# Weight slots returned to the front, rows scaled on ScalarE, and a fourth usual pair in a two-layer transformer kernel

## The chip, the cores and the metric

The kernel runs on one core of one Trainium2 chip. The metric is device time in microseconds (us) of one execution, median of the runs; lower is better.

## The reference

Two layers, each an attention block and then a gated block, on 2048 rows of 448 numbers, all in float32:

```python
x = A_x
x = x + attention(layernorm(x), wqkv, wo)          # 16 heads of 28
x = x + gated(layernorm(x), w_gate, w_up, w_down)
x = x + attention(layernorm(x), wqkv, wo)
x = x + gated(layernorm(x), w_gate, w_up, w_down)

def gated(x, w_gate, w_up, w_down):                # 448 -> 1792 -> 448
    return (sigmoid(x @ w_gate) * (x @ w_up)) @ w_down
```

The change touches the gated block of both layers, and only there its schedule.

## The kernel before

TensorE works in float16: each operand is split into a high and a low float16 part, and a product is the sum of three (high by high, low by high, high by low). The schedule is written out by hand: each engine executes its instructions in the order in which the program emits them, and the tile framework adds the waits between engines.

**The gated block.** The 2048 rows are cut into `NB = 4` blocks of 512, the 1792 hidden features into `NP = 7` pairs of 2 x 128. The loop `for b, p in seq` in `gated` runs over the 28 pairs of a layer, (0,0) to (3,6). For a pair `gate_and_up` computes gate and up products with a fast 2x2 scheme of seven products instead of eight: `first`, `second`, `third` write the two `chain` banks, which ScalarE copies out (`on_chain`, L1527); `apart` and `c11_c22`, `c12` write the two `side` banks, which VectorE adds (L1543, L1550); `c21` uses the chain banks again. In between stand six places, `along(0)` to `along(5)`, to which the list `at` assigns other work: the operands of the pair before (`Operands.parts`, `rest`), the down products of the block before (`pieces`), and preparation steps of a later block (`run_fill(steps, n)`, counts from `portions(b, p)`). 78 matmuls of 256 columns make a pair.

**The down product** uses the same scheme: seven products per pair, for block `b - 1` while block `b` goes through its pairs; in one pair of block b that is six matmuls of 224 columns for each pair of the block before. The last block's products follow in a stage of their own after the loop (the order is `TAIL`); it will be called the closing stage. The first `USUAL` pairs of block 0 go another way: their down product is done in the usual form (`down`, 24 matmuls of 448 columns, banks 0 to 3), emitted behind the next pair, and `add_usual` adds it to `x`. So TensorE's order in block 0 is pair 0, pair 1, down of 0, pair 2, down of 1, and so on.

**Preparing a block.** `Block.steps()` lists it: `norm` (mean and variance on VectorE, the power on GpSimd), `squares` (VectorE scales the rows and transposes 32x32 squares), `store` and `gather` (through DRAM, to complete the transpose, by SyncE's queue), and nine half steps `r11` to `last_rows`, in which VectorE subtracts and ScalarE rounds to float16. Block b + 1 is prepared in block b. In the first layer, the last block prepares two blocks for the next attention (`after`).

**Slots.** Large tiles take one of 19 equal slots of SBUF (`big`), quarter-sized ones one of 12 (`qrt`). `get` takes the slot at the front of the list of free ones, `put` appends the slot at its end. A tile whose slot had another tile before it waits for that tile's last reader. `WeightsGated` keeps two pairs of gate/up weights (two tiles of 800 KB each per pair, `load_gu`) and three tiles of down weights (784 KB, `load_dn`). `used_gu` and `used_dn`, called at the end of each pair (in the closing stage `used_dn` after each product), put the used slots and start the next load on GpSimd's queue. The closing stage begins like this; the load of the fourth product's weights is started by the first `used_dn` of the second loop:

```python
for n in range(3):
    pieces(b, TAIL[n], range(NP - 1), w[n], True)
for n in range(3):
    pieces(b, TAIL[n], [NP - 1], w[n])
    wt.used_dn()
    finish(b, TAIL[n])
for k in TAIL[3:]:
    ...
        pieces(b, k, range(NP), wt.dn[0])
```

Of the kernel before, what the change touches and what calls it, by code (L numbers as in the profile page):

```python
# [19 lines left out]
P = 128  # L20
S = 2048
D = 448
# [34 lines left out]
N_SUMS = 25  # L57
DN = D // 2
N_DN = 8
USUAL = 3  # L60
SHORT = ((10, 23, 12), (11, 24, 13), (8, 22, 9))
# [13 lines left out]
class Slots:  # L75
# [28 lines left out]
    def put(self, *tiles):  # L104
        for t in tiles:
            i, _ = self.held.pop(id(t))
            self.free.append(i)


@with_exitstack  # L110
def interleaved_layers(ctx: ExitStack, tc: tile.TileContext, x_in, wqkv, wo, w_gate, w_up,
# [143 lines left out]
    class Block:  # L255
# [15 lines left out]
        def norm(self, js=range(TB)):  # L271
            b = self.b
            if js[0] == 0:
                uid[0] += 1
                self.mv = cpool.tile([P, TB, 2], F32, name=f"mv_{uid[0]}", tag="mv", bufs=2)
                self.rs = cpool.tile([P, TB], F32, name=f"rs_{uid[0]}", tag="rs", bufs=2)
            for j in js:
# [6 lines left out]
                                    op1=ALU.mult)  # L284
            nc.gpsimd.tensor_tensor(rs, rs, nhalf[:, c], op=ALU.pow)

        def scale(self, j):
# [34 lines left out]
        def gather(self):  # L322
            rows = self.scr.rearrange("j r i n -> (j r) (i n)")
            self.raw = big.get("xraw", [P, 4, W])
            nc.sync.dma_start(self.raw[:, 0:3, :],
                              rows[0:384].rearrange("(k p) n -> p k n", p=P))
            nc.sync.dma_start(self.raw[0:64, 3, :], rows[384:D])
            if self.halves:
                nc.gpsimd.memset(self.raw[64:P, 3, :], 0.0)

# [12 lines left out]
        def steps(self):  # L343
            return self.squared() + [
                lambda: (self.store(), self.gather())] + (
                        self.half_steps() if self.halves else
                        [lambda: self.ready(0, 1), lambda: self.ready(2, 3)])

        def squared(self):
            return [lambda do=do, j=j: do((j,)) for do in (self.norm, self.squares)  # L350
                    for j in range(TB)]

        def half_steps(self):
# [43 lines left out]
            def r11():  # L397
                self.wide = big.get("xwide", [P, 4, 2, 2, W // 2], F16)
                self.short = big.get("xshort", [P, 3, 2, 2, W // 2], F16)
                self.t1 = subtract("t1", cut(0, 2), cut(0, 0))  # L400
                high(self.wide[:, 0], cut(0, 0))
# [51 lines left out]
        def begin(self):  # L453
            uid[0] += 1
            self.mv = cpool.tile([P, TB, 2], F32, name=f"mv_{uid[0]}", tag="mv", bufs=2)
            self.rs = cpool.tile([P, TB], F32, name=f"rs_{uid[0]}", tag="rs", bufs=2)
            self.xn = big.get("xn", [P, TB, D])
# [870 lines left out]
    class WeightsGated:  # L1328
# [26 lines left out]
        def load_dn(self, queue=nc.sync):  # L1355
            self.dn.append(big.get("dn", [P, NP, 2, DN], F16))
            queue.dma_start(self.dn[-1], dn_parts[self.products.popleft()])

        def used_gu(self):
            big.put(*self.gu.popleft())  # L1360
            if self.pairs:
                self.load_gu(nc.gpsimd)

        def used_dn(self):
            big.put(self.dn.popleft())
            if self.products:
                self.load_dn(nc.gpsimd)

    def gated(layer, first, wt, before_next):
# [237 lines left out]
        for b, p in seq:  # L1607
            if p == 0:
                if b + 1 < NB:
                    blks.append(Block(b + 1, True))  # L1610
                    steps.extend(blks[b + 1].steps())
                elif not last:
                    after = [Block(0), Block(1)]
                    blks.append(after[0])
                    steps.extend(after[0].steps())
# [12 lines left out]
            for i, n in enumerate(portions(b, p)):  # L1628
                at[i].append(lambda n=n: run_fill(steps, n))
            if b == 0 and p > USUAL or b == 1 and p == 0:  # L1630
                for j in range(TB)[p - USUAL - 1:p - USUAL] if b == 0 else range(
                        NP - USUAL - 1, TB):
                    at[0].append(lambda j=j: add_usual(j))
# [160 lines left out]
```

## Time and profile before

| | |
|---|---|
| median of 3 runs | 1913.93 us (1912.98 to 1913.96) |
| the profiled execution | 1918.24 us, its span 1916.4 us |
| TensorE clock in it | 0.997 of full speed |
| gated block, first layer, blocks 0 to 2 | from 605.6 to 850.3 us of the span |
| gated block, second layer, blocks 0 to 2 | from 1550.0 to 1796.4 us of the span |
| end of the second layer's closing stage | 1912.7 us of the span |

Times in the profile are microseconds from the span's start. PE is TensorE's matmuls, PEld its weight loads, DVE VectorE, ACT ScalarE, POOL GpSimd, SP SyncE; L545 is line 545 of the kernel. A matmul's duration covers its way through the array; the next one starts long before its end, so what one costs is the distance between starts. Pair boundaries are the first weight load of a pair on `gu_s`, counted off 78 to a pair; all 4368 are in the trace.

### The profile page before, as it was taken

What the parts mean: (1) busy time and instruction counts of PE and PEld (TensorE: products, weight loads), DVE (VectorE), ACT (ScalarE), POOL (GpSimd) and SP (SyncE); (2) the same over time, 40 slices, a digit from 0 to 9 for tenths busy, and PEclk for the clock granted to TensorE, in tenths of its full rate; (3) what the DMA queues carried; (4) which work ended last, traced back from release to release, by engine and by line L of the source; (5) the groups of instructions that cost most, each with busy time, mean ns of one, the idle gap of its engine ahead of it and who ended that gap; (6) DMA issues with size and microseconds to landing.
All of it is one profiled execution on the core that took longest, in us unless ns stands there. A gap on an engine that the chain in (4) does not pass through costs nothing. (4 is left out here: it accounts for less than half of the span.)

```text
span 1916.4 us, 56353 instructions
## 1 busy us (share of the span) xinstructions
PE 1897.9 (99%) x24317; PEld 1405.8 (73%) x24317; DVE 1412.8 (74%) x2816; ACT 1366.0 (71%) x1742; POOL 240.6 (13%) x467
## 2 busy tenths in 40 slices
PE   9999999999999999999999999999999999999999
PEld 4455655555566798999954568778888777899998
DVE  7648798687877598788663487778778667887764
ACT  5569999999983455454344799999999645555541
POOL 2013312232001111212100000000000011211110
PEclk9999999999999999999999999999999999999999
DMA  5575555345313657656634312122111235665752
GB/s 173 165 207 162 155 157 149 117 144 149 92 62 92 235 189 263 219 221 236 232 94 132 89 51 51 28 51 51 41 37 66 75 98 215 216 270 198 270 204 90
DMA packets 107298, 275.20 MB, mean 144 GB/s; under 512 B 12766, under 2 KB 63086, under 8 KB 106912
## 3 DMA queue, kind: packets, MB, share of 16 engines
q0 software_dynamic: 33088, 165.74, 24.5%
q1 hardware_dynamic: 73616, 105.54, 19.3%
q8 instruction: 192, 3.15, 0.7%
q14 instruction: 66, 0.54, 0.1%
q10 hardware_dynamic: 336, 0.23, 0.0%
HBM read 213.39 MB, written 50.73 MB: 138 GB/s over the span
## 5 line engine op out<-in xcount | busy, mean ns | idle before, releaser
L1144 ACT ACTIVATE prob_s<-sc 128x1536 f32<-128x1536 f32 x659 | 892.7, 1484 | 6.7 <-PE sc L1129 3.3
L1180 PE MATMUL acc<-prob_s,val_s 128*32 128x256 f32 (+3 forms) x7754 | 590.1, 383 | 0.0
L1129 PE MATMUL sc<-qp_s 114*32 114x512 f16 x7896 | 575.8, 379 | 0.0
L545 PEld LDWEIGHTS <-gu_s 128*128 128x128 f16 x4368 | 428.0, 98 | 60.3 <-issue 8.1
L1129 PEld LDWEIGHTS <-qp_s 114*32 114x32 f16 x8192 | 309.9, 96 | 176.3 <-issue 78.2
L1180 PEld LDWEIGHTS acc<-prob_s,val_s 128*32 128x32 f32 x7754 | 317.9, 110 | 100.8 <-issue 7.6
L545 PE MATMUL chain<-xwide_s,gu_s 128*128 128x256 f16 x2016 | 249.0, 273 | 4.1 <-DMA gu_s<-gu_parts 4.0
L1454 PE MATMUL dnp<-dn_s,hparts_s 128*128 128x224 f16 x2100 | 235.5, 259 | 0.0
L1454 PEld LDWEIGHTS <-hparts_s 128*128 128x128 f16 x2100 | 202.1, 98 | 4.8
L1527 ACT COPY one_q<-chain 128x256 f32<-128x256 f32 x224 | 82.0, 372 | 132.0 <-PE chain L545 131.3
L1160 DVE SCALAR_TENSOR_TENSOR power_q<-power_q,expo_q 128x512 f32<-128x512 f32 x222 | 153.7, 692 | 7.6
L545 PE MATMUL side<-xshort_s,gu_s 128*128 128x256 f16 x1120 | 142.1, 274 | 3.0 <-DVE one_q L1543 2.7
L530 PE MATMUL qkp<-xhl_s,wqk_s 128*128 128x512 f16 x616 | 138.0, 379 | 0.7 <-DVE xhl_s L509 0.3
L1543 DVE TENSOR_TENSOR one_q<-side,one_q 128x512 f32<-128x512 f32 x112 | 72.0, 684 | 83.4 <-PE side L545 83.4
L530 PEld LDWEIGHTS <-wqk_s 128*128 128x128 f16 x616 | 60.0, 98 | 70.1 <-ACT wqk_s L223 1.0
L1209 DVE STREAM_TRANSPOSE oturned_q<-acc 128x512 f32<-128x512 f32 x32 | 22.9, 717 | 118.4 <-PE acc L1180 118.4
L1345 POOL DMA_DIRECT2D gu_s<-gu_parts x104 | 56.0, 540 | 365.7 <-PE side L545 183.3
L545 PE MATMUL side<-xwide_s,gu_s 128*128 128x256 f16 x672 | 92.3, 274 | 0.0
L1407 ACT CAST hparts_s<-hsums_q 128x256 f16<-128x256 f32 (+1 forms) x144 | 68.4, 489 | 33.1 <-DVE hsums_q L1419 20.6
L722 ACT ACTIVATE qkhl_q<-qkp 128x512 f16<-128x512 f32 x56 | 33.2, 593 | 75.0 <-PE qkp L530 71.6
L1180 PE MATMUL acc<-power_q,val_s 128*32 128x256 f32 (+3 forms) x278 | 86.4, 393 | 0.0
L1554 ACT ACTIVATE one_q<-one_q 128x512 f32<-128x512 f32 x56 | 35.3, 630 | 71.3 <-DVE one_q L1543 71.2
(209 smaller groups left out, 2291.0 us busy)
## 6 DMA issues: line engine op xcount, KB each, us to landing
gu_s<-gu_parts POOLq DMA_DIRECT2D x104, 800.0 KB, 6.0
dn_s<-dn_parts POOLq DMA_DIRECT2D x50, 784.0 KB, 7.2
qp_s<-qk_scr SPq DMA_DIRECT2D x96, 224.0 KB
qk_scr<-qkhl_q SPq DMA_DIRECT2D x56, 256.0 KB
gu_parts<-pack_s POOLq DMA_DIRECT2D x14, 800.0 KB, 4.2
xt_scr<-xs_s SPq DMA_DIRECT2D x48, 224.0 KB
xraw_s<-xt_scr SPq DMA_DIRECT2D x12, 768.0 KB
qp_s<-qk_scr SPq DMA_DIRECT2D x64, 112.0 KB
```

What stands on the lines that cost most here:

```text
L530: nc.tensor.matmul(pm, w, x, start=(i == 0), stop=(i == len(terms) - 1))
L545: nc.tensor.matmul(pm, a, x, start=(first and i == 0), stop=(i == len(terms) - 1), skip_group_check=True)
L1129: nc.tensor.matmul(ps[32 * j:32 * j + 32, :], hd.k[:, keys], hd.q[:, qb * W:(qb + 1) * W], start=True, stop=True, tile_position=(0, 32 * j))
L1144: nc.scalar.activation(prob[:, 0:n, :], ps[:, 0:n, :], AF.Exp, scale=exp_scale)
L1160: nc.vector.scalar_tensor_tensor(p, p, c[k], y, op0=ALU.add, op1=ALU.mult)
L1180: nc.tensor.matmul(acc[qb * VC:(qb + 1) * VC, s], v[:, kc % TB, h, :], probs[c * NB + qb][:, s], start=(kc == 0 and a == 0), stop=(kc == N ...
L1345: queue.dma_start(self.gu[-1][m], gu_parts[p, m])
L1407: nc.scalar.copy(to[:, :, 0], a)
L1454: nc.tensor.matmul(pm, a[:, x, t], w[:, p, y], start=(begin and n == 0 and (j == 0 or alone)), stop=(n == 2), skip_group_check=True)
L1527: nc.scalar.copy(to, pm)
L1543: nc.vector.tensor_tensor(one[m], side[m], one[m], op=ALU.add)
L1554: nc.scalar.activation(out, v, AF.Sigmoid, scale=gate_scale)
```

## The change

It does five things.

- `put_next` puts slots back at the front of the free list; `used_gu` and `used_dn` use it, so that the next load of weights goes into the very slot just read.
- In the preparation VectorE no longer scales rows: `norm_one` adds two small GpSimd operations for an offset, `lift` has ScalarE compute scale times row plus offset into a quarter slot, and `square` has VectorE transpose it.
- Block 2's normalisation, transposition, `store` and `gather` move from block 1 to block 0's pairs; its half steps stay in block 1. Block 1's first half step moves from the second place of pair (0,2) to its last. `portions` is rewritten.
- `USUAL` is 4 instead of 3, with the times of `add_usual` in `AFTER_USUAL`. Block 1 then has three instead of four pairs of down products in each of its pairs, and the down weights for block 0 are loaded without their first four pairs.
- Two memsets on GpSimd move or go (`gather`, `t3`); `last_low` gets a small ScalarE copy of zeros.

```diff
-USUAL = 3
+USUAL = 4
+AFTER_USUAL = ((0, 5), (0, 5), (1, 0), (1, 2))
...
+    def put_next(self, *tiles):
+        for t in tiles[::-1]:
+            i, _ = self.held.pop(id(t))
+            self.free.appendleft(i)
...
+        def norm_one(self, j):
+            self.norm((j,))
...
+            nc.gpsimd.tensor_tensor(off, self.mv[:, j, 0:1], self.rs[:, j:j + 1], op=ALU.mult)
+            nc.gpsimd.tensor_scalar(off, off, -1.0, None, op0=ALU.mult)
+
+        def lift(self, j):
+            self.lifted[j] = qrt.get("lifted", [P, D])
+            nc.scalar.activation(self.lifted[j], x[:, self.b * TB + j, :], AF.Identity,
+                                 scale=self.rs[:, j:j + 1], bias=self.off[:, j:j + 1])
+
+        def square(self, j):
+            if j == 0:
+                self.xs = big.get("xs", [P, NQ, TB, 32])
+            if j + 1 < TB:
+                self.lift(j + 1)
+            v = self.lifted.pop(j)
+            nc.vector.transpose(self.xs[:, :, j, :], v)
+            qrt.put(v)
...
         def steps(self):
-            return self.squared() + [
-                lambda: (self.store(), self.gather())] + (
+            squared = self.squared()
+            return squared[:-1] + [
+                lambda: (squared[-1](), self.store(), self.gather())] + (
...
         def squared(self):
-            return [lambda do=do, j=j: do((j,)) for do in (self.norm, self.squares)
-                    for j in range(TB)]
+            return [lambda j=j: self.norm_one(j) for j in range(TB)] + [
+                lambda: self.lift(0)] + [lambda j=j: self.square(j) for j in range(TB)]
...
-                nc.gpsimd.memset(self.t4[64:P, 1, :], 0.0)
...
+                nc.scalar.copy(self.short[64:P, 1, 1, 1], self.raw[64:P, 3, 0:W // 2])
...
         def load_dn(self, queue=nc.sync):
-            self.dn.append(big.get("dn", [P, NP, 2, DN], F16))
-            queue.dma_start(self.dn[-1], dn_parts[self.products.popleft()])
+            t = big.get("dn", [P, NP, 2, DN], F16)
+            first = USUAL if len(self.products) > NP * (NB - 1) else 0
+            queue.dma_start(t[:, first:], dn_parts[self.products.popleft(), :, first:])
+            self.dn.append(t)

         def used_gu(self):
-            big.put(*self.gu.popleft())
+            big.put_next(*self.gu.popleft())
...
         def used_dn(self):
-            big.put(self.dn.popleft())
+            big.put_next(self.dn.popleft())
...
-        blks = [first]
-        steps = deque()
+        blks = [first] + [Block(b, True) for b in range(1, NB)]
+        s1, s2 = blks[1].steps(), blks[2].steps()
+        ahead = 2 * TB + 1
+        steps = deque(s1[:ahead] + s2[:TB] + s1[ahead:] + s2[TB:ahead])
...
         if b == 0:
-            steps = {0: {1: 4, 5: 5}, 2: {1: 1, 2: 1, 3: 1, 5: 1}, 3: {1: 1, 2: 1, 3: 1, 5: 1},
-                     4: {1: 1}}
-        elif b < NB - 1:
-            steps = {0: {1: 2, 2: 1}, 1: {1: 2, 2: 1}, 2: {1: 1, 2: 2}, 3: {5: 1},
-                     4: {1: 1, 3: 1}, 5: {1: 1, 3: 1}, 6: {1: 1, 2: 1, 3: 1, 5: 1}}
+            steps = {0: {1: 4, 3: 1, 5: 4}, 2: {1: 2, 2: 2, 5: 1}, 3: {1: 1, 2: 2, 3: 1, 5: 1},
+                     4: {1: 1, 2: 1, 3: 2, 5: 2}, 5: {1: 2}}
+        elif b == 1:
+            steps = {1: {1: 1, 5: 1}, 2: {2: 1}, 3: {1: 1, 5: 1}, 4: {5: 1}, 5: {1: 1, 5: 1},
+                     6: {2: 1}}
+        elif b == 2:
+            steps = {0: {1: 2, 2: 2}, 1: {1: 2, 2: 1, 5: 2}, 3: {2: 1, 5: 1}, 4: {1: 1, 5: 1},
+                     5: {1: 1, 2: 1, 5: 1}, 6: {1: 1, 3: 1}}
         else:
-            steps = {0: {1: 2, 2: 1}, 1: {1: 2, 2: 1}, 2: {1: 1, 2: 2}, 3: {1: 2, 2: 2},
-                     4: {1: 1, 2: 1}, 5: {1: 1, 2: 1}, 6: {1: 1, 2: 2, 5: 1}}
+            steps = {0: {1: 2, 2: 1}, 1: {1: 2, 2: 1}, 2: {1: 2, 2: 2}, 3: {1: 2, 2: 2},
+                     4: {1: 2, 2: 1}, 5: {1: 1, 2: 1}, 6: {1: 1, 2: 2, 5: 2}}
```

More of the change, by code (lines that the diff above doesn't have):

```diff
@@ L274, in norm @@
                 uid[0] += 1
-                self.mv = cpool.tile([P, TB, 2], F32, name=f"mv_{uid[0]}", tag="mv", bufs=2)
-                self.rs = cpool.tile([P, TB], F32, name=f"rs_{uid[0]}", tag="rs", bufs=2)
+                self.mv = cpool.tile([P, TB, 2], F32, name=f"mv_{uid[0]}", tag="mv", bufs=4)
+                self.rs = cpool.tile([P, TB], F32, name=f"rs_{uid[0]}", tag="rs", bufs=4)
             for j in js:
@@ L285, in norm @@
             nc.gpsimd.tensor_tensor(rs, rs, nhalf[:, c], op=ALU.pow)
+        def norm_one(self, j):
+            self.norm((j,))
+            if j == 0:
+                self.off = cpool.tile([P, TB], F32, name=f"off_{uid[0]}", tag="off", bufs=4)
+                self.lifted = {}
+            off = self.off[:, j:j + 1]
+            nc.gpsimd.tensor_tensor(off, self.mv[:, j, 0:1], self.rs[:, j:j + 1], op=ALU.mult)
[5 more added lines that the diff above has]
+        def square(self, j):
+            if j == 0:
+                self.xs = big.get("xs", [P, NQ, TB, 32])
[4 more added lines that the diff above has]
+            qrt.put(v)
         def scale(self, j):
@@ L399, in r11 @@
                 self.short = big.get("xshort", [P, 3, 2, 2, W // 2], F16)
+                if not self.turned:
+                    nc.gpsimd.memset(self.raw[64:P, 3, :], 0.0)
                 self.t1 = subtract("t1", cut(0, 2), cut(0, 0))
@@ L1608, in gated @@
             if p == 0:
-                if b + 1 < NB:
-                    blks.append(Block(b + 1, True))
+                assert b == 0 or not steps
+                if b == 1:
+                    steps.extend(s2[ahead:])
+                elif b == 2:
                     steps.extend(blks[b + 1].steps())
-                elif not last:
+                elif b == NB - 1 and not last:
                     after = [Block(0), Block(1)]
-                    blks.append(after[0])
                     steps.extend(after[0].steps())
@@ L1629, in gated @@
                 at[i].append(lambda n=n: run_fill(steps, n))
-            if b == 0 and p > USUAL or b == 1 and p == 0:
-                for j in range(TB)[p - USUAL - 1:p - USUAL] if b == 0 else range(
-                        NP - USUAL - 1, TB):
+            for j in range(TB):
+                if AFTER_USUAL[j] == (b, p):
                     at[0].append(lambda j=j: add_usual(j))
```

7 lines of the change are left out of this document (3 added, 4 removed).

## The prediction

> **What bounds the kernel now.** I read the page first, then the waits of TensorE, then busy times by pair of the gated loop.
>
> ```profile
> span 1916.4 us, 56353 instructions
> PE 1897.9 (99%) x24317; PEld 1405.8 (73%) x24317; DVE 1412.8 (74%) x2816; ACT 1366.0 (71%) x1742; POOL 240.6 (13%) x467
> PE chain L545 <- DMA gu_s<-gu_parts: 4.0, 2, 2.1
> PE chain L545 <- ACT one_q L1527: 3.6, 2, 2.5
> PE side L545 <- DVE one_q L1543: 2.7, 2, 2.0
> ```
>
> TensorE sets the time; nothing else can gain except where it waits or does less. Its long waits are few: weights that land late, and chain or side banks that ScalarE and VectorE free late, each once per layer. Where, and what they cost with all that follows, the busy times by stage tell (length, busy PE, PEld, DVE, ACT, POOL, granted clock, DMA share, GB/s):
>
> ```profile
> 627.36:645.50 18.14, 14.80 (x103) 10.57 (x102) 9.56 (x22) 6.74 (x16) 2.41 (x5) 0.91 0.43 149
> 645.50:658.56 13.06, 13.06 (x104) 9.98 (x103) 7.46 (x19) 7.55 (x20) 0.57 (x2) 1.00 0.79 292
> 658.56:667.15 8.59, 8.59 (x79) 7.62 (x78) 4.98 (x12) 4.68 (x13) 1.07 (x2) 1.00 0.78 317
> 684.20:762.48 78.28, 76.17 (x716) 69.39 (x714) 68.85 (x154) 43.58 (x108) 15.48 (x32) 1.00 0.63 223
> 727.89:740.85 12.96, 10.98 (x104) 9.86 (x103) 9.95 (x23) 6.44 (x16) 1.59 (x3) 1.00 0.76 298
> 740.85:762.48 21.63, 21.63 (x206) 19.84 (x205) 19.56 (x44) 14.23 (x35) 4.00 (x8) 1.00 0.61 230
> 1571.78:1589.93 18.15, 15.11 (x104) 10.51 (x103) 9.76 (x22) 6.73 (x16) 2.70 (x6) 0.91 0.42 151
> 1628.63:1708.66 80.03, 77.83 (x717) 70.27 (x715) 68.85 (x154) 43.58 (x108) 15.48 (x32) 0.98 0.63 224
> 1672.32:1687.03 14.71, 12.65 (x105) 10.72 (x103) 9.95 (x23) 6.44 (x16) 1.59 (x3) 0.88 0.68 265
> ```
>
> Rows 1 and 7 are pair (0,2) with the usual down product of pair 0 behind it, in the first and second layer; row 2 is the same work in pair (0,3), undisturbed: 5.1 us are lost per layer. Row 3 is a pair alone, 8.59. Rows 4 and 8 are the seven pairs of block 1. Two undisturbed pairs there take 21.63 (row 6), 10.82 each; seven would take 75.7, so 2.6 and 4.3 us are lost, mostly in pair (1,4) (rows 5 and 9). The same wait costs 2.1 us at full clock in row 5 and 3.9 in row 9, where the clock fell to 0.88: a lowered clock is worth about 1.75 us.
>
> The timelines of VectorE and GpSimd in the second layer show what (0,2) waits for.
>
> ```profile
> 1564.55 0.53 POOL L1345 DMA_DIRECT2D gu_s<-gu_parts  x1 [7.88 <-DVE xs_s L305]
> 1574.07 1.05 POOL L1345 DMA_DIRECT2D gu_s<-gu_parts  x2 [9.00 <-DMA xt_scr<-xs_s]
> 1578.52 0.76 DVE L371 TENSOR_TENSOR t_q<-xraw_s 128x256 f32<-128x256 f32 x2 [8.15 <-DMA xraw_s<-xt_scr]
> 1581.67 0.42 DVE L371 TENSOR_TENSOR t_q<-xraw_s,t_q 128x256 f32<-128x256 f32 x1 [1.39 <-DMA xraw_s<-xt_scr]
> 1582.02 1.28 DVE L1543 TENSOR_TENSOR one_q<-side,one_q 128x512 f32<-128x512 f32 x2
> 1668.03 7.21 DMA gu_s<-gu_parts
> ```
>
> VectorE sits in `r11` until the rows of block 1 are back from DRAM, and only then frees the side bank. Weight loads wait for a slot that `xs` still holds; the last row (chain of waits) is such a load, landing at 1675.24 for pair (1,4), which began at 1672.32.
>
> **What the change takes away.** In (0,2), `r11` moves from the second place to the last, so nothing in that pair waits for the rows, and ScalarE doing the scaling sends them off earlier. Its next deadline is pair (0,3), a usual down product (4.5 us) later. I take the whole 5.1 per layer: **-10.2**. In block 1 three product pairs stand in each pair instead of four; six matmuls of 224 columns cost 0.57 (row below), so a pair falls from 10.82 to 10.25. With weights in their own slots no load waits for `xs`, whose work has also left block 1. Seven pairs: 71.7 instead of 78.3 and 80.0: **-14.9**.
>
> **What it adds on TensorE.** One more usual down product per layer, row 2 less row 3, 4.5 us: **+9.0**. The scheme with seven products is given up for that pair, so this trade alone costs 0.5 per layer.
>
> **Closing stage.** Here I look at what the old order of slots gave. Rows of the chain of waits, GpSimd's timeline and the down weights (last one: around 935 to 942 us):
>
> ```profile
> 1869.69 1.09 PE side L545 x10
> 1873.25 0.57 PE dnp L1454 x6
> 1883.33 29.34 PE dnp L1454 x306
> ...
> 1870.54 1.08 POOL L1357 DMA_DIRECT2D dn_s<-dn_parts  x2 [10.31 <-PE side L545]
> 1872.23 0.53 POOL L1357 DMA_DIRECT2D dn_s<-dn_parts  x1 [0.62 <-PE dnp L1454]
> ...
> DMA to landing us min/median/max: 4.4/6.6/7.4
> ...
> DMA to landing us min/median/max: 4.8/12.0/17.7
> ```
>
> The 306 matmuls of row 3 run without a gap: twelve belong to pair (3,6), the other 294 are the closing stage, 0.096 us each. Its weights were all on their way by 1872.23, twelve microseconds ahead, because `get` handed out slots that gate/up weights had left. With `put_next` the load for the fourth product takes the slot of the first, so it waits for the last reader of that: product 1's seventh pair. From there TensorE has twelve matmuls left, 1.15 us. The load is issued 0.3 after the last reader (five of row 1's ten matmuls end at 1870.24, the issue is at 1870.54) and takes 4.4 alone (the smallest of the three landings; the later two stood behind another). So TensorE waits 0.3 + 4.4 - 1.15, about 3.6 us per layer: **+7.2**. The fifth to seventh loads have a product of 42 matmuls (4.0) more cover each and land in time. In the first layer the next layer's weights move at the same time; the third product's load, issued at the stage's start, must land within 72 matmuls, 6.9 us. By the last two rows it takes between 4.4 and 12.0, a wait of 0 to 5.1; it is a single load, so I take **+0.5**.
>
> **ScalarE in pair (0,0).** Its last place now holds three `lift`s, emitted ahead of the two float16 copies for the down product and of the copy that frees chain bank 0 for the next pair.
>
> ```profile
> 1559.03 0.42 ACT L1554 ACTIVATE two_q<-two_q 128x256 f32<-128x256 f32 x1 [1.16 <-DVE two_q L1550]
> 1559.36 0.60 ACT L210 CAST hhl_q<-one_q 128x512 f16<-128x512 f32 x1
> 1559.94 0.62 ACT L210 CAST hhl_q<-two_q 128x512 f16<-128x512 f32 x1
> 1560.47 0.64 ACT L1527 COPY one_q<-chain 128x256 f32<-128x256 f32 x2
> ...
> L1407 ACT CAST hparts_s<-two_q 128x256 f16<-128x256 f32 x50 | 20.2, 404 | 0.0
> L223 ACT ACTIVATE wqk_s<-wraw_s,up 128x384 f16<-128x384 f32 x1 | 0.6, 599 | 0.0
> L223 ACT ACTIVATE wqk_s<-wraw_s,up 128x256 f16<-128x256 f32 x1 | 0.5, 507 | 1.2 <-DVE up L240 1.2
> L288 DVE TENSOR_SCALAR xn_s<-x,mv,rs 128x448 f32<-128x448 f32 x64 | 31.2, 498 | 4.8 <-POOL rs L285 3.5 <-POOL rs L466 1.0
> ```
>
> ScalarE has no idle time there, so every microsecond ahead of 1560.47 is TensorE's. No `lift` is in the trace. L223 scales by a per-row operand: 507 and 599 ns for 256 and 384 columns, by that slope 645 for 448; a second per-row operand (the offset) may add as much as the first did, 507 - 404, making 750. Instructions in a row start 0.08 before their predecessor ends. Three cost 1.7 to 2.0; I take 1.85 per layer: **+3.7**. They replace VectorE's 0.50 each, where VectorE was not what TensorE waited for. The Trainium skill (ScalarE: Activation LUTs, What ACT_TABLE_LOAD costs) gives about 93 ns for each such operand, and a lift would then take 745 ns, an estimate from that page; L223 agrees with 103 for one, and by the page the term is +4.0. The same page's Rules for kernel authors would leave multiply and add to VectorE, which speaks against this move, and the rows 498 against 645 to 750 agree.
>
> **Two half steps in one place of (0,3).** `t2` and `t3` both stand in the third place: VectorE's low part in `t3` needs ScalarE's high part of `t2`, which comes behind the copies of `third`.
>
> ```profile
> L381 ACT CAST xwide_s<-t_q 128x512 f16<-128x512 f32 x24 | 14.9, 620 | 6.6 <-DVE t_q L367 4.0 <-DVE t_q L371 2.5
> L390 DVE TENSOR_TENSOR xwide_s<-t_q,xwide_s 128x512 f16<-128x512 f32 x24 | 16.4, 682 | 0.0
> L371 DVE TENSOR_TENSOR t_q<-xraw_s,t_q 128x256 f32<-128x256 f32 x24 | 9.2, 418 | 1.7 <-DMA xraw_s<-xt_scr 1.7
> ```
>
> With matmuls of 256 columns at 0.109 (1.09 for ten, above), `third` ends 5.2 us into the pair, its copies at 5.8, the high part at 6.4 (0.62), the low part at 7.1 (0.68), `t4` at 7.8 (two of 0.42), and the side bank's sum 0.65 later, 8.4; `c12` would want it at 7.4. One microsecond per layer: **+2.0**; none, if ScalarE runs ahead of this count.
>
> **At nothing**, with cover: GpSimd's two more small operations per tile (13% busy), its memsets, the zero copy in `last_low` (ScalarE, places without a deadline), `lift`s in blocks 2 and 3 (pairs of 10 to 12.5 us, ScalarE busy about half), block 2's preparation in (0,4) and (0,5) (behind the extra down product), `add_usual` (VectorE, banks not needed before block 1 and later), GpSimd's load issue, now always behind the pair's end. In block 3 of the first layer `ready` comes one place earlier against its `gather`; up to 1.5 us if it lands late.
>
> **Sum of the waits**: -10.2 - 14.9 + 9.0 + 7.2 + 0.5 + 3.7 + 2.0 = -2.7.
>
> **The clock.** New waits of 3.6, 1.9 and 1.0 us per layer follow. Rows 5 and 9 show two waits of some 2.1 us, one with and one without the fall; rows 1 and 7 one with in each layer (0.91), after waits of more than 3 us together. So I count a fall for both closing stages, 1.4 each, since part of it passes in the wait, and one of the two after (0,0), 1.75: +4.55, and in all **+1.85**. The Trainium skill (TensorE: Matmul & The Clock Gate, The HAM clock gate) has the clock fall after an idle window of about 3.4 us; then these waits would hardly lower it, and the time would be that of case (e) below. Row 9 disagrees (a fall after 2.1 us), so I keep the rows.
>
> On the profiled execution that is 1918.24 + 1.85 = 1920.1 us; it stood 4.3 above the median, and the same difference on the median gives 1913.93 + 1.85 = **1915.8 us**. What a measurement can tell from no change is 0.2%, 3.8 us.
>
> **Rivals.** (a) Slower, by the clock: it falls after all four long waits, 1.75 each, +7.0 on -2.7: 1918.2. It leaves the 0.2% once clock falls cost over 6.5. For it speaks row 9, against it row 5. (b) Slower, by the weights: a load now starts only when its pair ends. In (0,6) the next must land in 8.6, plus 0.65 to the first use of the up half, less 0.5 for its later issue, 8.7 us. While rows went through DRAM two such loads took
>
> ```profile
> DMA to landing us min/median/max: 8.1/8.8/9.5
> ```
>
> and block 2's rows now travel just there. From 8.7 on it decides: 0.8 more and a fall of 1.75 per layer, +5.1 on the forecast: 1920.9. Against it: only the second of the two loads came that late. (c) Faster: the waits in (0,0) and (0,3) do not come, since ScalarE is idle earlier than I count: -2.7 - 5.7 and falls of 2.8 at the end: 1908.3. Against it speaks ScalarE's gapless row of 1559 to 1561. (d) The slots do not return as `put_next` says and the closing stage runs on: -2.7 - 7.7 + 1.75: 1905.3. (e) No fall at all: the sum of the waits alone, 1911.2; row 5 speaks for it, rows 1, 7 and 9 against.
>
> **Chances.** Forecast 0.33, (e) or part of the falls 0.10, (a) 0.22, (b) 0.15, (c) 0.13, (d) 0.07. Within 0.2% are the forecast and (e), 0.43; slower 0.37; faster 0.20. The forecast's own range is 1912 to 1918; with (a), (b), (c) and their open bounds (5.1 in the closing stage, 1.5 in `ready`) it is 1907 to 1923.
>
> **What would show it.** Right: pairs (0,2) near 13.1, block 1 near 10.25 per pair; a wait `PE dnp <- DMA dn_s` of about 3.6 in each closing stage; (0,1) longer by 1.9 behind L1527; (0,3) longer by 1.0 behind L1543; clock under 1 behind them. Wrong: a closing stage without a gap, which would leave the change faster, or waits for `gu_s` in blocks 0 and 1, which would make it clearly slower.

## Result and the profile after

The changed kernel takes 1931.65 us (median; 1930.14 to 1934.12), the kernel before beside it 1913.45 us: 1.0096 times as long, 95% interval 1.0079 to 1.0114. The forecast was 1915.8 us, in a range of 1907 to 1923. The profiled execution took 1934.12 us with a span of 1932.4, against a span of 1916.4 before: 16.0 us more. By the medians it is 18.2 us. The two profiled executions stood above their medians by different amounts (1934.12 against 1931.65, 1918.24 against 1913.93), so what follows adds up the 16.0 us between the two spans; which waits the median executions had more or less of, no trace shows.

Head of the page and top of TensorE's waits (us in total, times, longest):

```profile
span 1932.4 us, 56301 instructions
PE 1903.2 (98%) x24281; PEld 1321.0 (68%) x24281; DVE 1392.8 (72%) x2768; ACT 1386.3 (72%) x1772; POOL 253.8 (13%) x523
PE dnp L1492 <- DMA dn_s<-dn_parts: 11.8, 3, 4.1
PE side L579 <- DVE one_q L1581: 5.2, 5, 3.1
PE chain L579 <- ACT one_q L1565: 3.8, 2, 1.9
```

The busy time of VectorE fell by 20 us and that of ScalarE rose by 20, as the scaling moved from one to the other; neither total explains the longer time. The first wait is new: TensorE stands before a down product three times for weights, 11.8 us in all. Next, the stages that the prediction spoke of, from the busy times by stage (length, then busy time of PE, PEld, DVE, ACT, POOL, granted clock, DMA share, GB/s):

```profile
614.01:629.07 15.06, 13.14 (x105) 10.06 (x103) 10.92 (x24) 7.85 (x17) 3.08 (x6) 1.00 0.78 249
629.07:642.13 13.06, 13.06 (x104) 10.00 (x103) 7.62 (x19) 5.20 (x13) 5.69 (x18) 1.00 0.52 188
642.13:656.19 14.06, 13.27 (x104) 9.97 (x103) 8.90 (x20) 7.27 (x17) 1.06 (x2) 1.00 0.33 123
686.46:758.83 72.37, 72.10 (x675) 65.45 (x673) 62.49 (x138) 44.26 (x110) 12.22 (x23) 1.00 0.57 212
1645.00:1717.81 72.81, 72.10 (x675) 65.41 (x673) 62.50 (x138) 44.45 (x110) 12.23 (x23) 1.00 0.58 215
884.33:901.79 17.46, 14.36 (x122) 12.60 (x121) 11.10 (x25) 6.65 (x15) 5.28 (x16) 0.90 0.60 208
939.40:980.30 40.90, 33.00 (x298) 30.80 (x297) 8.69 (x16) 0.92 (x2) 2.64 (x5) 0.87 0.49 188
1893.40:1928.60 35.20, 31.26 (x297) 29.72 (x294) 8.65 (x16) 0.93 (x2) 2.64 (x5) 0.90 0.40 148
```

Rows 1 to 3 are pairs (0,1), (0,2) and (0,3) of the first layer: the wait of 5.1 us in (0,2) is gone (13.06), (0,1) is 1.87 longer than the 13.19 it had before (the row below), (0,3) 1.0 longer. Rows 4 and 5 are block 1 in both layers, 72.4 and 72.8 instead of 78.3 and 80.0. Up to here it went as forecast. Row 6 is pair (3,3) of the first layer, 12.54 in the kernel before. The last two rows cover most of the closing stages; from the last gate matmul to the end they take 41.87 and 36.17 us, where both took 29.34 before. In row 7 TensorE is idle for 40.90 - 33.00 = 7.9 us, and its 298 matmuls take 33.00 instead of 298 x 0.096 = 28.6, since the clock fell to 0.87. Row 8: 3.9 us idle, 2.75 lost to the clock.

Pair (0,1) of the first layer in the kernel before:

```profile
614.17:627.36 13.19, 13.13 (x104) 9.97 (x102) 11.14 (x23) 5.99 (x14) 0.55 (x1) 1.00 0.60 170
```

The lowered clock, in three stretches of the changed kernel's busy times, two in the first layer's closing stage and one in the second's:

```profile
949.29:956.12 6.83, 5.47 (x30) 4.32 (x30) 0.00 (x0) 0.00 (x0) 0.00 (x0) 0.50 0.29 120
962.95:966.36 3.41, 3.41 (x21) 2.77 (x19) 0.00 (x0) 0.00 (x0) 0.00 (x0) 0.50 0.69 285
1908.44:1915.26 6.82, 5.63 (x31) 4.56 (x32) 0.00 (x0) 0.00 (x0) 0.00 (x0) 0.50 0.59 237
```

The granted clock is one half for 6.83, 3.41 and 6.82 us. Of the two long stretches 1.36 and 1.19 us still lie in the waits, which ended at 950.65 and 1909.63 and in which TensorE had nothing to run. Half of what is left, 2.7, 1.7 and 2.8 us, is what the three falls cost, some 7.2 us in all.

| change of the span, us | forecast | measured |
|---|---|---|
| pair (0,2), both layers | -10.2 | -10.2 |
| block 1, both layers | -14.9 | -13.1 |
| one more usual product | +9.0 | +8.9 |
| lifts in (0,0), seen in (0,1) | +3.7 | +3.7 |
| `t2` and `t3` in one place of (0,3) | +2.0 | +2.0 |
| clock after (0,0) | +1.75 | 0 |
| closing stages with their clock | 7.7 + 2.8 = +10.5 | 12.5 + 6.8 = +19.4 |
| `ready` in block 3, pair (3,3) | 0 | +4.9 |
| the rest | 0 | +0.4 |
| sum | +1.85 | +16.0 |

The closing stage of the first layer in TensorE's timeline, and the loads it waits for in GpSimd's (start, length, operation, in brackets the idle time before and what ended it). The two lines after them are the landing times of the third product's load, 939.97 in the first layer and its twin at 1893.92 in the second:

```profile
938.36 8.21 PE L1492 MATMUL dnp<-dn_s,hparts_s 128*128 128x224 f16 x84
950.65 7.98 PE L1492 MATMUL dnp<-dn_s,hparts_s 128*128 128x224 f16 x54 [4.08 <-DMA dn_s<-dn_parts]
962.45 17.93 PE L1492 MATMUL dnp<-dn_s,hparts_s 128*128 128x224 f16 x168 [3.81 <-DMA dn_s<-dn_parts]
...
939.97 0.53 POOL L1392 DMA_DIRECT2D dn_s<-dn_parts  x1 [12.01 <-PE dnp L1492]
957.78 1.68 POOL L1392 DMA_DIRECT2D dn_s<-dn_parts  x3 [17.28 <-PE dnp L1492]
...
DMA to landing us min/median/max: 10.6/10.6/10.6
...
DMA to landing us min/median/max: 4.5/4.5/4.5
```

The wait of 3.81 is the fourth product, issued at 957.78: the forecast's mechanism, with 3.6 expected (3.9 in the second layer, where the load, issued at 1904.85, took 4.74). The wait of 4.08 is the third product. Its load starts at the same point of both layers, and takes 4.5 us in the second layer, where only the output's rows move beside it, and 10.6 in the first, where rows for the next layer's attention and its weights move too.

### The profile page after: what moved, and what is told of

Its sections match the earlier page's. It is cut to its first block, busy times and chain, and to the rows that moved or that the text cites. A ratio compares the mean times of both kernels' runs of the same rounds, so it can differ in the third digit from the quotient of the medians.

```text
span 1932.4 us, 56301 instructions
## 1 busy us (share of the span) xinstructions
PE 1903.2 (98%) x24281; PEld 1321.0 (68%) x24281; DVE 1392.8 (72%) x2768; ACT 1386.3 (72%) x1772; POOL 253.8 (13%) x523
## 5 line engine op out<-in xcount | busy, mean ns | idle before, releaser
L1214 PE MATMUL acc<-prob_s,val_s 128*32 128x256 f32 (+3 forms) x7754 | 568.8, 383 | 0.0
L1163 PE MATMUL sc<-qp_s 114*32 114x512 f16 x7896 | 553.7, 379 | 0.0
L579 PEld LDWEIGHTS <-gu_s 128*128 128x128 f16 x4368 | 427.2, 98 | 59.0 <-issue 10.6
L1163 PEld LDWEIGHTS <-qp_s 114*32 114x32 f16 x8192 | 265.5, 95 | 213.7 <-issue 101.4
L1214 PEld LDWEIGHTS acc<-prob_s,val_s 128*32 128x32 f32 x7754 | 269.5, 110 | 146.2 <-issue 11.7
L1492 PE MATMUL dnp<-dn_s,hparts_s 128*128 128x224 f16 x2016 | 233.4, 265 | 11.8 <-DMA dn_s<-dn_parts 11.8
```

Source lines behind the costliest of these rows:

```text
L579: nc.tensor.matmul(pm, a, x, start=(first and i == 0), stop=(i == len(terms) - 1), skip_group_check=True)
L1163: nc.tensor.matmul(ps[32 * j:32 * j + 32, :], hd.k[:, keys], hd.q[:, qb * W:(qb + 1) * W], start=True, stop=True, tile_position=(0, 32 * j))
L1214: nc.tensor.matmul(acc[qb * VC:(qb + 1) * VC, s], v[:, kc % TB, h, :], probs[c * NB + qb][:, s], start=(kc == 0 and a == 0), stop=(kc == N ...
L1492: nc.tensor.matmul(pm, a[:, x, t], w[:, p, y], start=(begin and n == 0 and (j == 0 or alone)), stop=(n == 2), skip_group_check=True)
```

## Experiments

Each is compared with the kernel before, run beside it.

**1. Down weights back to the old order** (`dn_put`), in the whole layer.

```diff
         def used_dn(self):
-            big.put_next(self.dn.popleft())
+            big.put(self.dn.popleft())
```

> The changed kernel with one line undone: the down weights' slots go to the end of the free list again (gate/up weights keep returning to the front). Theory (own slots): the closing stages lose 12.5 and 6.8 us only because a load waits for the last reader of its own slot. Then both last about 29.4 us again, no wait of PE dnp for DMA dn_s, and the time is 1931.65 - 19.4 = 1912.3 us. Rival (contention): loads in the closing stage land late because the next layer's weights move at the same time (10.6 us for one load in the trace). Then only the two waits of the fourth product go, with their clock, and the first layer keeps its wait for the third product: about 1918.5 us.

1915.86 us, 1.0007 (0.9997 to 1.0017). Both closing stages are 29.34 long again without a gap; the first, in the busy times by stage:

```profile
938.41:967.75 29.34, 29.34 (x309) 29.33 (x307) 9.60 (x19) 1.86 (x4) 4.69 (x13) 1.00 0.67 264
```

So the 19.4 us of the closing stages come from this one line of the change. The total came 3.6 above the expected 1912.3. By the spans (1932.4 to 1915.0) it is 2.0 too much: (2,3), where VectorE waits for block 3's rows in `r11`, took 14.04 and 13.76 where it had taken 12.64 and 12.54, while (3,3) was 16.07 for 17.46. The other 1.6 are that the profiled execution of the changed kernel stood 2.5 us above its median, and this one 0.9.

**2. The same only in the closing stage** (`closing_put`): the two calls of `used_dn` there put the slot at the end.

```diff
-            wt.used_dn()
+            wt.used_dn(big.put)
```

> The changed kernel, with the old way of giving slots back only in the four calls of the closing stage. Own slots: the wait for the fourth product (3.98 and 4.1 us, with the clock after it) goes in both layers; the load of the third product is still issued at the end of pair (3,6) into its own slot, so its wait in the first layer stays: 1931.65 - 12.9, about 1918.7 us, the first layer's closing stage about 35.5 us, the second's 29.4. Rival (the third product's wait and the fourth's are one late chain, and the later loads make room for the third): the first layer's stage also falls to 29.4, 1912 us.

1921.36 us, 1.0037 (1.0023 to 1.0052), between the two, 2.7 above the expectation (by the spans 0.8: 12.1 of the 12.9 us came). The second layer's closing stage is whole (29.34); the first takes 36.38 and has one wait for down weights left in TensorE's waits:

```profile
PE dnp L1492 <- DMA dn_s<-dn_parts: 4.1, 1, 4.1
```

It is the third product. Its load is started before the closing stage, by the `used_dn` of the last pair, and there the slot still came from `put_next`. Two waits with two causes, then, told apart: the fourth product by its slot in the stage, the third by its slot in the pair before.

**3. The new order of the down weights in the old kernel** (`before_dn_next`): the kernel before with `put_next` for the down weights alone.

> The kernel before with one line of the change alone: the down weights' slots return to the front. Own slots: both closing stages get the waits of the changed kernel (third and fourth product in the first layer, fourth in the second, some 4 us each, and the clock after them), 41.9 and 36.2 us instead of 29.3; blocks 0 to 2 as before: 1914.25 + 19.4, about 1933 us. Rival (it needs the rest of the change, as the gate/up weights' slots no longer serve): less than +5 us.

1931.08 us, 1.0091 (1.0074 to 1.0108). With nothing else changed, the closing stages grow to 39.03 and 34.72 us:

```profile
PE dnp L1460 <- DMA dn_s<-dn_parts: 10.1, 3, 3.9
```

The same three waits. The stages are shorter than the expected 41.9 and 36.2, as the waits are shorter (10.1 us for 11.8) and each of the three falls of the clock lasted 3.41 us. By the medians this line alone costs 17.1 us, nearly the 18.2 of the whole change.

**4. TensorE kept busy in the closing waits** (`closing_busy`): the changed kernel with unneeded matmuls of 512 columns into a spare bank where TensorE would wait (17 before the third product in the first layer, 16 before the fourth). Only the clock can gain by it.

```diff
+            if n == 2 and not last:
+                stir(17)
             pieces(b, TAIL[n], range(NP - 1), w[n], True)
...
+        stir(16)
         for k in TAIL[3:]:
```

> The changed kernel with matmuls on data that nobody uses put where PE waited in the closing stages (17 and 16 of 512 columns in the first layer, 16 in the second, 3.5 us each at full clock). They take no work away. If a lowered clock after the idle time costs 4.3 and 2.7 us beyond the waits themselves, it stays at full speed and the closing stages fall to some 37.5 and 33.5 us: 1931.65 - 7 = 1924.7 us. If the waits alone cost the time, nothing changes: 1931.65 us or more.

1927.84 us, 1.0081 (1.0063 to 1.0099). Its closing stages in the busy times, and TensorE's waits for down weights:

```profile
938.93:976.41 37.48, 36.80 (x342) 32.47 (x340) 9.53 (x19) 1.86 (x4) 2.64 (x5) 1.00 0.55 206
1888.25:1921.76 33.51, 32.96 (x324) 30.81 (x322) 9.52 (x19) 1.86 (x4) 2.64 (x5) 1.00 0.42 153
...
PE dnp L1492 <- DMA dn_s<-dn_parts: 1.2, 3, 0.6
```

The clock stays at 1.00 and the stages are 4.4 and 2.65 us shorter, though TensorE still waits for the loads at the end of each run of unneeded matmuls (1.2 us in all): 7 of the 19.4 us are the clock, the rest is the waiting itself. That is 4.4 us for the two falls of the first layer and 2.7 for the one of the second, against the 1.4 per stage that I had put down. The span gained 6.6 us, the median 3.8 where 7 were expected.

**5. The rows of the next attention later** (`ready_later`): in block 3 the first `ready` moves from the third place of (3,3) to the second place of (3,4), where it stood before.

```diff
-            steps = {0: {1: 2, 2: 1}, 1: {1: 2, 2: 1}, 2: {1: 2, 2: 2}, 3: {1: 2, 2: 2},
-                     4: {1: 2, 2: 1}, 5: {1: 1, 2: 1}, 6: {1: 1, 2: 2, 5: 2}}
+            steps = {0: {1: 2, 2: 1}, 1: {1: 2, 2: 1}, 2: {1: 2, 2: 2}, 3: {1: 2, 2: 1},
+                     4: {1: 2, 2: 2}, 5: {1: 1, 2: 1}, 6: {1: 1, 2: 2, 5: 2}}
```

> The changed kernel with the first ready step of the next attention's block 0 moved from the third place of pair (3,3) to the second of (3,4), where it stood before. Theory (rows not back yet): ScalarE waited 4.0 us for xraw in (3,3), PE 3.3 us for the side bank, and the clock fell; now (3,3) and (3,4) last 12.54 us each, 4.9 less: 1926.7 us. Rival (the rows land so late that the wait only moves on): 1931.7 us, with the wait in (3,4).

1930.18 us, 1.0081 (1.0064 to 1.0098), where 1926.7 was expected; by the medians alone it can't be told from the changed kernel. But pairs (3,3) and (3,4) are 12.54 each, so the 4.9 us of (3,3) are this move's. The span gained only 2.2, mostly because (2,3), whose code is unchanged, took 13.51 and 13.70 in this execution against 12.64 and 12.54. What the changed kernel does in (3,3), in SyncE's, GpSimd's and ScalarE's timelines; the last line is ScalarE's part of `ready` in the kernel before, whose pair (3,3) began at 887.88:

```profile
885.12 0.38 SPq L358 DMA_DIRECT2D xraw_s<-xt_scr  x1
883.19 1.17 POOL L1379 DMA_DIRECT2D gu_s<-gu_parts  x2 [2.65 <-PE side L579]
884.89 0.53 POOL L1392 DMA_DIRECT2D dn_s<-dn_parts  x1 [0.53 <-PE dnp L1492]
895.39 1.14 ACT L218 CAST xhl_s<-xraw_s 128x512 f16<-128x512 f32 x2 [4.00 <-DMA xraw_s<-xt_scr]
...
904.84 1.14 ACT L210 CAST xhl_s<-xraw_s 128x512 f16<-128x512 f32 x2
```

The gather is issued at 885.12, behind two weight loads and just behind a third; ScalarE gets the rows at 895.39, 10.3 us later, and has stood idle for 4.0 us in `ready`, with the side bank's copies behind it. In the kernel before the same cast came 17.0 us after the pair's start, here it was due 7.1 after it (895.39 less the 4.0 it waited, pair start 884.33): ten microseconds earlier.

**6. Experiments 1 and 5 together** (`dn_put_ready`).

> Both of dn_put and ready_later. If the two losses are independent they add: 1931.65 - 19.4 - 4.9 = 1907.3 us, below the kernel before (1913.45). If they share a cause (the memory traffic around the end of the first layer) the sum falls short: 1910 to 1912 us.

1911.56 us, 0.9987 (0.9977 to 0.9996): the two faults taken out of the change, what is left is a little faster than the kernel before. It is 4.3 us less than experiment 1, so here the later `ready` shows in the medians too. Its remaining waits:

```profile
PE chain L579 <- ACT one_q L1565: 3.8, 2, 1.9
PE side L579 <- DVE one_q L1581: 2.6, 5, 0.8
```

The lifts in (0,0), 1.9 per layer, and side banks, with `t3` in (0,3) among them. Expected were 1907.3. On the spans, 22.7 of the 24.3 us came (1932.4 to 1909.7); (2,3) with 13.24 and pair (1,0) with 11.41 in the second layer, where gate/up weights land late, took 1.1 of the rest. The medians lie closer together than the spans by 2.6: the profiled execution of the changed kernel stood 2.5 above its median, this one 0.1 below its own.

**7. Gate/up weights to their own slots in the kernel before** (`before_gu_next`).

> The kernel before, with the gate/up weights' slots alone returning to the front. Theory: pair (1,4) waited for weights whose slot xs still held; that wait goes (2.1 and 3.9 us), pair (0,2) keeps its 18.1 us, the closing stages 29.3: about 1908 us. Rival (b) of the prediction: loads that start only when their pair ends land late where rows go through DRAM; (1,4) or its neighbours keep a wait, 1912 us or more.

1934.09 us, 1.0098 (1.008 to 1.0115), where a gain or no change was expected. Pair (1,4) grew from 13 and 15 us to 22.8 and 22.3, at a clock of 0.78. Around the rows of block 2, in the timelines of SyncE, GpSimd and ScalarE; first the kernel before, then this one, with its row of (1,4) in the busy times on top:

```profile
713.70 2.31 SPq L317 DMA_DIRECT2D xt_scr<-xs_s  x4
723.27 0.38 SPq L325 DMA_DIRECT2D xraw_s<-xt_scr  x1
713.97 0.53 POOL L1345 DMA_DIRECT2D gu_s<-gu_parts  x1 [6.82 <-DVE xs_s L305]
723.70 0.53 POOL L1345 DMA_DIRECT2D gu_s<-gu_parts  x1 [9.20 <-DMA xt_scr<-xs_s]
728.02 0.69 ACT L379 CAST xwide_s<-xraw_s 128x256 f16<-128x256 f32 x2
```

```profile
729.71:752.51 22.80, 13.55 (x105) 11.14 (x103) 10.04 (x23) 6.35 (x16) 1.59 (x3) 0.78 0.40 148
...
715.63 3.00 SPq L323 DMA_DIRECT2D xt_scr<-xs_s  x4
730.13 0.38 SPq L331 DMA_DIRECT2D xraw_s<-xt_scr  x1
717.75 1.07 POOL L1351 DMA_DIRECT2D gu_s<-gu_parts  x2 [8.58 <-PE side L551]
718.82 0.53 POOL L1363 DMA_DIRECT2D dn_s<-dn_parts  x1
728.57 1.07 POOL L1351 DMA_DIRECT2D gu_s<-gu_parts  x2 [9.22 <-PE side L551]
740.15 0.71 ACT L385 CAST xwide_s<-xraw_s 128x256 f16<-128x256 f32 x2 [10.22 <-DMA xraw_s<-xt_scr]
```

In the kernel before, the second weight load stands at its slot until the rows' store is through (`xs` holds it, 9.20 us), so the rows go to DRAM beside one load and their gather goes ahead of the next; ScalarE has them by 728.02, 14.3 us after the store began. With own slots three loads go out with the store and two more ahead of the gather, and the rows come back 24.5 us after the store began (740.15 less 715.63). The wait for the slot, which the forecast counted as a loss, was also what gave the rows the queues.

**8. The same with `r11` later** (`gu_next_late`): in blocks 1 and 2 the first half step moves from the last place of (b,3) to the last of (b,4).

```diff
-            steps = {0: {1: 2, 2: 1}, 1: {1: 2, 2: 1}, 2: {1: 1, 2: 2}, 3: {5: 1},
-                     4: {1: 1, 3: 1}, 5: {1: 1, 3: 1}, 6: {1: 1, 2: 1, 3: 1, 5: 1}}
+            steps = {0: {1: 2, 2: 1}, 1: {1: 2, 2: 1}, 2: {1: 1, 2: 2}, 3: {},
+                     4: {5: 1}, 5: {1: 1, 2: 1, 3: 1, 5: 1}, 6: {1: 1, 2: 1, 3: 1, 5: 1}}
```

> The kernel before with only the gate/up weights returned to their own slots, and in blocks 1 and 2 the first half step r11 moved from the last place of pair (b,3) to the last place of pair (b,4) (the others closer together behind it). Theory (weight loads that no longer wait for a slot meet the rows' way through DRAM, and the rows come back some 9 us later, while VectorE stands in r11): the rows land at about 740 us of the span, and r11 now begins at about 738, so pair (1,4) falls from 22.8 and 22.3 us to about 10.9 and the wait of 9 us goes; some 22 us are won back on 1934.1, and 1911 us results if the closer half steps cost a microsecond or so. Rival (the loads of weights are themselves late, or VectorE has too much to do): (1,4) or (1,5) stays near 20 us, 1928 us or more.

1911.64 us, 0.9985 (0.9976 to 0.9995). SyncE's gather, VectorE's first use of the rows, and the busy times of (1,4):

```profile
726.12 0.38 SPq L331 DMA_DIRECT2D xraw_s<-xt_scr  x1
...
737.77 0.75 DVE L377 TENSOR_TENSOR t_q<-xraw_s 128x256 f32<-128x256 f32 x2
...
725.69:736.51 10.82, 10.82 (x105) 9.94 (x104) 7.73 (x16) 5.52 (x14) 1.59 (x3) 1.00 0.84 312
```

The store still lasts until 726.12 (it began at 711.62), 14.5 us as in experiment 7, but nobody asks for the rows before they are there, and (1,4) is undisturbed. The half steps that now stand closer cost 0.7 us per layer in (1,6), 11.51 for 10.82. In this kernel own slots pay only together with a later reader. That is what the change did for block 2's rows (prepared a block ahead) and not for block 3's or for `ready`.

**9. VectorE scales the rows again** (`vector_scale`, on `dn_put_ready`).

```diff
-            nc.scalar.activation(self.lifted[j], x[:, self.b * TB + j, :], AF.Identity,
-                                 scale=self.rs[:, j:j + 1], bias=self.off[:, j:j + 1])
+            nc.vector.tensor_scalar(self.lifted[j], x[:, self.b * TB + j, :],
+                                    self.mv[:, j, 0:1], self.rs[:, j:j + 1],
+                                    op0=ALU.subtract, op1=ALU.mult)
```

> dn_put_ready with the rows scaled by VectorE again (subtract and multiply, in the place of each lift). ScalarE theory: three lifts ahead of the copy that frees chain bank 0 cost pair (0,1) 1.87 us per layer; (0,1) returns to 13.2 us and the time falls by 3.7 to 1907.9 us. Rival (VectorE has no room for them): (0,1) is shorter, but waits of PE for VectorE appear in (0,2), (0,4) to (1,0), and the time stays at 1911 us or above.

1908.65 us, 0.9972 (0.9963 to 0.9982), 2.9 us less than experiment 6. Pair (0,1) is 13.41 instead of 15.06:

```profile
613.82:627.23 13.41, 13.14 (x105) 9.99 (x103) 12.37 (x27) 5.99 (x14) 3.10 (x7) 1.00 0.83 255
```

VectorE is busier there (12.4 of 13.4 us) than ScalarE was with the lifts (7.9 of 15.1), and yet it costs TensorE 0.2 instead of 1.9: the busy share does not decide. Whether the engine does, or the place in its order of work, the next two tell apart.

**10 and 11. Places instead of engines.** `places` is `dn_put_ready` with the lifts of (0,0) spread (two in its fifth place, the last in (0,1)), `t3` from the third to the fourth place of (0,3) and block 3's `r11` from the third to the fourth place of (2,3). `vector_places` is `vector_scale` with the last two of these.

```diff
-        steps = deque(s1[:ahead] + s2[:TB] + s1[ahead:] + s2[TB:ahead])
+        early = [lambda: (blks[1].lift(1), blks[1].lift(2))]
+        steps = deque(s1[:TB + 1] + early + s1[TB + 1:ahead] + s2[:TB] + s1[ahead:] +
+                      s2[TB:ahead])
...
-            steps = {0: {1: 4, 3: 1, 5: 4}, 2: {1: 2, 2: 2, 5: 1}, 3: {1: 1, 2: 2, 3: 1, 5: 1},
+            steps = {0: {1: 4, 3: 1, 4: 1, 5: 2}, 1: {0: 2}, 2: {1: 2, 2: 2, 5: 1},
+                     3: {1: 1, 2: 1, 3: 2, 5: 1},
...
-            steps = {0: {1: 2, 2: 2}, 1: {1: 2, 2: 1, 5: 2}, 3: {2: 1, 5: 1}, 4: {1: 1, 5: 1},
+            steps = {0: {1: 2, 2: 2}, 1: {1: 2, 2: 1, 5: 2}, 3: {3: 1, 5: 1}, 4: {1: 1, 5: 1},
```

> The changed kernel with used_dn by put and the rows of block 3 read one pair later (as dn_put_ready, 1911.6), and three more places moved: the lifts of pair (0,0) earlier (two in its fifth place, the last in pair (0,1)), t3 of block 1 from the third to the fourth place of (0,3), r11 of block 3 from the third to the fourth place of (2,3). Theory (each remaining excess is an instruction in a place too early or too late for the engine that TensorE waits for): (0,1) from 15.06 to 13.1, (0,3) from 14.06 to 13.06, (2,3) to about 12.5, that is 1911.6 - 3.7 - 2.0 - 0.7 = about 1905.3 us. Rival (ScalarE has no spare time anywhere in (0,0) and (0,1), so the lifts cost the same elsewhere): (0,1) or (0,0) stays 1.9 us too long, 1909 us.

> As dn_put_ready, with the rows scaled by VectorE in place of ScalarE's lifts (vector_scale, 1908.7), and t3 of block 1 one place later in (0,3), r11 of block 3 one place later in (2,3). Theory: (0,3) from 14.06 to 13.06 in each layer, (2,3) from 12.9 and 13.7 to about 12.5: 1908.7 - 2.0 - 0.8 = about 1905.9 us. Rival (VectorE has no slack in (0,3), so t3 delays the side bank from any place): (0,3) stays at 14, 1908 us.

`places` takes 1904.40 us, 0.9941 (0.9925 to 0.9958), `vector_places` 1904.88 us, 0.9946 (0.993 to 0.9963): both faster than the kernel before and the changed one, and not to be told from each other. In `places`, (0,1), (0,3), (3,3) and the first closing stage:

```profile
614.32:627.53 13.21, 13.13 (x104) 9.98 (x102) 10.90 (x24) 7.09 (x16) 3.09 (x7) 1.00 0.84 247
640.59:653.64 13.05, 13.05 (x103) 9.97 (x102) 8.20 (x19) 7.17 (x17) 1.06 (x2) 1.00 0.36 129
881.68:894.22 12.54, 12.54 (x122) 11.65 (x121) 9.96 (x23) 5.63 (x13) 5.25 (x16) 1.00 0.74 269
930.68:960.02 29.34, 29.34 (x309) 29.33 (x307) 9.52 (x19) 1.86 (x4) 4.71 (x13) 1.00 0.69 264
...
PE chain L579 <- DMA gu_s<-gu_parts: 1.3, 1, 1.3
```

Every pair is at its undisturbed length but (1,0) (10.52 and 11.71; the last line, from TensorE's waits, is its late gate/up weights) and (1,2) (0.47, where `add_usual` stands; not tried by itself). Once the lifts stand where nobody waits behind them, these runs show no difference between the engines that scale.

## Why the prediction was wrong

In blocks 0 and 1 the prediction found the places and the causes, and four of its terms hold within 0.1 us: (0,2), the usual product, the lifts, `t3`, and with them the cost of an instruction that stands ahead of the one TensorE waits for. That (0,2) fits so closely is in part luck: it was read from one execution, and in the two variants of the kernel before whose (0,2) has the same code (experiments 3 and 7) it took from 17.3 to 19.2 us. A lift takes 755 ns by its group in ScalarE's rows:

```profile
L307 ACT ACTIVATE lifted_q<-x,off,rs 128x448 f32<-128x448 f32 x32 | 23.3, 755 | 0.0
```

That is 5 ns over the upper bound from L223's rows. Three lifts held ScalarE for 2.05 us and put the copy behind them off by 1.87; that the middle of 1.7 to 2.0 hit this was luck. The estimate of 745 ns from the Trainium skill (ScalarE: Activation LUTs, What ACT_TABLE_LOAD costs) agrees within 10 ns. The rule in the Trainium skill (ScalarE: Activation LUTs, Rules for kernel authors) that leaves multiply and add to VectorE was right for the place of the change (experiment 9) and made no difference that shows once the place was right (10 and 11).

Two steps failed: the closing stage with its clock, and `ready` put at nothing. They make up 13.8 of the 14.2 us between +1.85 and +16.0.

**The closing stage, 8.9 us too little.** The fourth product's wait was right in cause (experiments 1 to 3) and near in size: 3.8 and 3.9 for 3.6, since the load took 4.6 to 4.7 instead of the 4.4 of the quietest of three landings. The third product's load was the bad choice: between the ends 0 and 5.1 I took 0.5, "it is a single load", and 4.08 was measured. The row with a median of 12.0 lay in front of me, from the same microseconds of the same layer. A single load was slow there too, so the number of loads was no reason to choose the low end. That the other traffic of that stretch made it slow is read from the same load's 4.5 us in the second layer; it was not tried by itself. Third, the clock: 7 us instead of 2.8 (experiment 4). I had counted two falls of 1.4 us. There were three, since the third product's wait brought its own, and two of them lasted twice as long as the 3.41 us of the shortest, so that they cost 2.7 and 2.8 although a part of each passed in the wait.

**`ready`, 4.9 us too little.** I put it among the edits "at nothing", as "one place earlier against its gather", with a bound of 1.5 us. It is five places: from the second place of (3,4) to the third of (3,3), ten microseconds by the trace. I had compared the counts of one pair in `portions` and not added up both lists from the start of the block, where the gather has kept its place (the third of (3,2)) and the reader has not. The rows then took 10.3 us to land behind weight loads; TensorE stood for 3.1 (row 6 of the stages, length less busy time) and lost the other 1.8 to the clock. Experiment 5 took all of it away.

**Smaller ones.** Block 1 gained 13.1 instead of 14.9: (1,0) loses 0.2 to 0.6 us to late gate/up weights, which is rival (b)'s cause in another pair, and (1,2), where `add_usual` stands, is 0.47 longer per layer, which I had put at nothing. Pair (0,6), where (b) expected its wait, lost 0.4 us in one layer, but behind VectorE (L1588) and not for weights. The clock did not fall after the wait of 1.9 us behind the lifts (row 1 of the stages, 1.00), which gave 1.75 back. Rival (d), that the closing stage runs on, is refuted by its own row; (a), more falls of the clock, was the right direction with the wrong places; (e), no fall, is right for the waits in (0,1) and (0,3) alone.

**The range** ended at 1923 because I took the open bounds singly. Added up, they reach 1927 (4.6 more for the third product, 1.5 for `ready`, 5.1 for rival (b)); the measured time lay outside even so, by `ready` and the clock.

**The clock by row and rule.** Waits of 1.9 and 0.8 us left the clock at 1.00 in (0,1) and (0,3); the 3.1 us in (3,3) and the 3.8 to 4.1 us in the closing stages lowered it, to 0.87 to 0.90 over those stages. The Trainium skill (TensorE: Matmul & The Clock Gate, The HAM clock gate) has it fall after an idle window of about 3.4 us, to half, and return after a busy window as long. By that page of the Trainium skill a fall costs 1.7 to 3.4 us, an estimate (half of one to two windows). The traces agree: half clock for 3.41, 6.82 or 6.83 us, at a cost of 1.7 to 2.8. As a threshold they do not bear it out: 3.1 us sufficed here, and 2.1 in one of two cases before.

## What to carry to other kernels

A load that waits for a slot may be what keeps the memory queues free for something more urgent: before handing the slot back earlier, list what is in flight in that stretch, and price every reader that stands just behind it with the landing times of that stretch, not with the quietest of the trace. Returning a slot to the front of a free list trades the start of the next load from "any time" to "after the last reader"; where the loop ends and no work is left to cover it, append instead. Price a TensorE wait of over 3 us with 2 to 3 us of lowered clock on top; here each of four cost 1.7 to 2.8.

## What the runs showed that I had not expected

- The way of 512 rows through DRAM took 14.3 us at most in the kernel before and 24.5 us when only the slot order of the gate/up weights was changed (experiment 7): with three loads of 784 to 800 KB beside the store and two ahead of the gather the rows came 10 us later, and (1,4) with its clock became 7.6 to 9.8 us longer.
- The same 784 KB load took 4.5 us in one layer and 10.6 us in the other.
- The granted clock fell to one half for stretches of 3.41 or 6.83 us, and a wait of 2.1 us was once enough for it.
- The pair (2,3), which waits for block 3's rows, took from 12.54 to 14.04 us over the executions of the changed kernel and of its variants with the same places there; with `r11` one place later it took 12.54 in both layers of both kernels. A reader that stands just at the landing makes the time vary as well as long.
